# Attention and two dense layers on one core: score tiles of two banks, the last 128 keys of two heads in a common bank, values per query tile in three pieces

## The chip, the core and the metric

The kernel runs on one core of a Trainium2 chip. The metric is the device time of one execution in microseconds (us); the kernel before takes 677.83 us, the median of three executions (676.55 to 678.01). Of the core's engines, PE is TensorE (PEld its weight loads), DVE is VectorE, ACT is ScalarE, POOL is GpSimd and SP is SyncE, which issues most DMAs. Each engine works through its own instructions strictly in the order in which the program issues them; semaphores hold one that needs another engine's result. PSUM has eight banks, each of 512 fp32 values per partition.

## The reference

Pooled attention for 2 x 8 heads of 1152 keys and 576 pooled queries of 64 values, and then two dense layers:

```python
q_pool = q.reshape(B, H, S // 2, 2, D).mean(axis=3)
scores = scale * np.matmul(q_pool, k.transpose(0, 1, 3, 2))
scores = scores - np.max(scores, axis=-1, keepdims=True)
attn = np.exp(scores)
attn = attn / (np.sum(attn, axis=-1, keepdims=True) + 1e-09)
x = np.matmul(attn, v)            # to (1152, 512)
h = x @ w_in                      # 512 -> 2048
g = np.maximum(h, 0.0) + np.log1p(np.exp(-np.abs(h)))
x = g @ w_out                     # 2048 -> 512
h = np.maximum(np.maximum(x @ w1, x @ w2), x @ w3)    # 512 -> 768
out = h @ w_out2                  # 768 -> 512
```

## The kernel before

Heads go in eight pairs. A pair has nine score tiles of 128 rows: four query tiles of 128 for each of its two heads (t = 0 to 3, head i = 0 and 1), and one tail tile that holds the last 64 queries of both. Tile m runs from 0 to 71, nine to a pair.

For each tile, `scores` (L437) makes three PSUM banks of 384 keys each with two matmuls a bank (three in the tail tile); the high and low halves of the operands are kept apart for accuracy. Two such score tiles fit at once (`NS` = 2), six banks. `key_max` (L453) takes the negated maximum over the 1152 keys on DVE, `exps` (L459) makes e = exp(s + nm) on ACT together with the row sum. `turn_e` (L472) transposes e in three groups of three 128 x 128 blocks (`te`), each into one of the two common banks (`NTB` = 2), and `keep_e` (L478) copies each group to `p` in SBUF, on DVE or ACT by the table `ENGINE`.

After four tiles (t = 0 and 1) and after the other five, `finish` (L614) closes a half pair w: `inverse` (L496) makes the reciprocals of the sums, `spread` (L505) spreads them over partitions with matmuls into a common bank (`tr`), `keep_spread` (L530) copies that to `rr`, `values` (L518) multiplies p with v in one run of matmuls into the other common bank (`x`), 256 columns wide for the first half pair and 320 for the second, and `divide` (L541) writes x times rr to `xy`. In `values` and `spread` each head writes one half of the partitions, so their matmuls load 64 columns of weights and two run at once; all other attention matmuls load 128.

While a pair runs, the next one is prepared (`prepare`, L555): q and k are loaded, q is pooled on POOL, both are transposed (`tq`, `tk`) through common banks and split into halves.

The order of all this is not written by hand. Each step is given to `Order.add` (L61) with an engine, a cost and a place (a number of tiles), and `Order.ordered` (L76) plays the steps through: an engine that is free takes the ready step of the lowest place. A step with `take` needs a free common bank, one with `free` gives it back. The instructions are issued in that order.

The conversion of the first ten weight tiles of the dense layers into high and low halves, and the first steps for three more, have places far behind everything else (L635 to L646), so they fill gaps. For each tile n there is a load `raw`, an absolute value on ACT (`size`), a bound on POOL, three integer steps on DVE (L237, L246, L250, into `t`), the high half on ACT (`wh`, L265) and the low half on DVE (`wl`, L270). The first three loads wait for the last keys and queries of the seventh pair, so the conversions begin late in the attention. The dense layers are ordered by a second `Order`, behind all of the above. Their first matmuls are five steps `up` (`bank_h`), and then `down` (`bank_y`), which needs the low half `gl` of the first hidden block from DVE (`low_g`, L755).

Of the kernel before, what the change touches and what calls it, by code (L numbers as in the profile page):

```python
# [8 lines left out]
F32 = mybir.dt.float32  # L9
# [3 lines left out]
ALU = mybir.AluOpType  # L13
# [3 lines left out]
P = 128  # L17
# [7 lines left out]
NBANKS = 7  # L25
NG = 8
NS = 2
NTB = 2
NE = 3

AT = {"max": -1.78, "exp": -0.31, "turn": 0.93, "keep": 0.1, "spread": 4.0, "values": 5.26}
ENGINE = ["DAA", "DDD", "DAA", "DDA", "ADD"]
PREP = {1: -5.28, 2: -7.74, 3: -4.5, 4: -3.31, 5: -1.64}
PREP_AFTER = {0: (0,), 1: (1, 2), 2: (3,), 3: (4,), 4: (5,)}


# [91 lines left out]
def kernel(  # L130
# [153 lines left out]
    def slot(name, n, count):  # L284
        return f"{name}{n % count}"
# [151 lines left out]
    def scores(m, pr, i, t, b):  # L437
        if b == 0:
            tiles["s", m] = ps.tile([P, NB, 512], F32, tag=slot("s", m, NS), name=f"s_{m}")
        sp = tiles["s", m]  # L440
        q1, q2, k1, kl = q1s[pr % 2], q2s[pr % 2], tiles["k1", pr], tiles["kl", pr]
        cols = slice(b * BK, (b + 1) * BK)
        to = sp[:, b, :BK]
# [9 lines left out]
    def key_max(m):  # L453
        tiles["nm", m] = sm.tile([P, 1], F32, tag=slot("nm", m, 3), name=f"nm_{m}")
# [4 lines left out]
    def exps(m, w, x, first):  # L459
        e = pp.tile([P, S], F32, tag=slot("e", m, NE), name=f"e_{m}")  # L460
        if first:
            tiles["sum", w] = sm.tile([P, 5], F32, tag=slot("sum", w, 2), name=f"sum_{w}")
        nc.scalar.activation(  # L463
            out=e.rearrange("p (b s) -> p b s", b=NB),
            in_=tiles["s", m][:, :, :BK],
            func=AF.Exp,
            bias=tiles["nm", m],
            accum_out=tiles["sum", w][:, x : x + 1],
        )
        tiles["e", m] = e  # L470
# [7 lines left out]
    def keep_e(w, i, t, b, n, first, engine):  # L478
        if first:
            tiles["p", w, b] = pp.tile([P, 2, KT, 2 * QB + TAILQ], F32, tag=f"p{b}", name=f"p_{w}_{b}")  # L480
        tp = tiles["t", n]
        if t < NT:
            c0 = (t % 2) * QB
            to = tiles["p", w, b][:, i, :, c0 : c0 + QB]
        else:
            to = tiles["p", w, b][:, :, :, 2 * QB :]
# [6 lines left out]
    def width(w):  # L493
        return 2 * QB if w % 2 == 0 else 2 * QB + TAILQ

    def inverse(w):  # L496
        nx = 4 if w % 2 == 0 else 5
        r = sm.tile([P, 5], F32, tag=slot("r", w, 2), name=f"r_{w}")
        tiles["r", w] = r
        nc.vector.tensor_scalar(  # L500
            out=r[:, :nx], in0=tiles["sum", w][:, :nx], scalar1=1e-9, scalar2=None, op0=ALU.add
        )
        nc.vector.reciprocal(r[:, :nx], r[:, :nx])

    def spread(w, n):  # L505

        r = tiles["r", w]
        tp = bank(n, [P, width(w)], f"tr_{w}")
        for t in range(2):
            for i in range(2):  # L510
                one = r[:, 2 * t + i : 2 * t + i + 1].to_broadcast([P, D])
                nc.tensor.matmul(tp[halves(i), t * QB : (t + 1) * QB], one, ident, start=True, stop=True)
        if w % 2:
            for i in range(2):
                one = r[:, 4:5].to_broadcast([P, D])
                nc.tensor.matmul(tp[halves(i), 2 * QB :], one, ident[:, halves(i)], start=True, stop=True)

    def values(w, n):  # L518
        x = bank(n, [P, width(w)], f"x_{w}")
        for j in range(NJ):  # L520
            for i in range(2):
                nc.tensor.matmul(  # L522
                    x[halves(i)],
                    tiles["v", w // 2][:, i, j],
                    tiles["p", w, j // KT][:, i, j % KT, : width(w)],
                    start=(j == 0),
                    stop=(j == NJ - 1),
                )
# [26 lines left out]
    def prepare(pr, step):  # L555
# [19 lines left out]
        else:  # L575
# [8 lines left out]
            elif g == NB - 1:  # L584
                order.add("SP", 5.6, p, both_k, pr, reads=[f"kh_{b}" for b in range(NB)],
                          writes=[f"k1{y}_{to}{b}" for to in range(2) for b in range(NB)])

    def one_tile(pr, x):
        i, t = (x % 2, x // 2) if x < 2 * NT else (0, NT)
        m = TILES * pr + x  # L590
        w = 2 * pr + (t >= 2)
        y = pr % 2
        sx = 2 * (t % 2) + i if t < NT else 4
        s, e = slot("s", m, NS), slot("e", m, NE)
        banks = [f"{s}_{b}" for b in range(NB)]
        for b in range(NB):
            order.add("PE", 0.35 if t < NT else 0.52, m + b / NB, scores, m, pr, i, t, b,
                      reads=[f"q{z}{y}_{g}" for z in (1, 2) for g in range(2)]
                      + [f"q1{y}_d0", f"q1{y}_d1", f"k1{y}_0{b}", f"k1{y}_1{b}", f"kl{y}_{b}"],
                      writes=(banks[b],) + ((s,) if b == 0 else ()))  # L600
        order.add("DVE", 1.28, m + AT["max"], key_max, m, reads=banks + [s], writes=(slot("nm", m, 3),))
        order.add("ACT", 1.21, m + AT["exp"], exps, m, w, sx, sx == 0,
                  reads=[slot("nm", m, 3), s] + banks, writes=(e, f"sum{w % 2}"))
# [7 lines left out]
        if sx == 3 and t == 1 or t == NT:
            finish(m, w)

    def finish(m, w):  # L614
        nx = 4 if w % 2 == 0 else 5
        y = (w // 2) % 2
        at = m + AT["values"]
        n1, n2 = next_bank(), next_bank()
        order.add("DVE", 0.3, m + 0.3, inverse, w, reads=(f"sum{w % 2}",), writes=(f"r{w % 2}",))
        order.add("PE", 0.6, m + AT["spread"], spread, w, n1, reads=(f"r{w % 2}",), writes=(f"b{n1}",), take=("t", n1))  # L620
        order.add("ACT", 0.36, m + AT["spread"], keep_spread, w, n1, reads=(f"b{n1}",), writes=("rr",), free=("t", n1))
        order.add("PE", 4.0 if w % 2 == 0 else 4.9, at, values, w, n2,
                  reads=[f"p_{x}_{b}" for x in range(nx) for b in range(NB)] + [f"v{y}"],
                  writes=(f"b{n2}", "pw"), take=("t", n2))
        order.add("DVE", 0.4, at - 3, divide, w, n2, reads=(f"b{n2}", "rr"), free=("t", n2))
# [372 lines left out]
```

## Time and profile before

| | |
|---|---|
| median of three executions | 677.83 us (676.55 to 678.01) |
| profiled execution, first to last instruction | 675.7 us |
| attention, to the last `divide` | 309.4 us of it |
| PE busy | 637.5 us, 94% |
| DVE busy | 446.9 us, 66% |
| ACT busy | 351.5 us, 52% |
| POOL busy | 219.6 us, 32% |

The profile gives no other time for the profiled execution than its span. What lies around a span is 2.1 us against the median. In the trace a matmul's row lasts from its start to the modelled end of its pipeline, so rows overlap; what a matmul costs in a run of them is the step from its start to the start of the next. DVE and ACT rows overlap a little in the same way.

### The profile page before, as it was taken

To read this page: it belongs to the slowest core of one execution; us is meant where nothing else is said; L and a number is where in the kernel's file an instruction comes from. 1 tells how busy PE (TensorE), PEld (TensorE's weight loads), DVE (VectorE), ACT (ScalarE), POOL (GpSimd) and SP (SyncE) were. 2 spreads that over 40 slices of the span, in tenths; PEclk is the share of its full clock that TensorE was granted. 3 is DMA by queue.
4 is the path that set the end of the run, shared out by engine and by line. 5 is a ranking of instruction groups with operands and counts; after the bars stand their busy time and mean duration, and the time that the engine had idled before them with its cause. 6 is when DMAs were issued, how large, how long until landed. Compare 5 with 4: busy or idle time off the path is not lost.

```text
span 675.7 us, 10352 instructions
## 1 busy us (share of the span) xinstructions
PE 637.5 (94%) x3914; PEld 556.3 (82%) x3914; DVE 446.9 (66%) x747; ACT 351.5 (52%) x697; POOL 219.6 (32%) x204
## 2 busy tenths in 40 slices
PE   2899999999999998999899999999999999999997
PEld 1676677676767766667799999999999999999996
DVE  3866667667777799985867979797688871111111
ACT  4655555556565666656767676767574431211211
POOL 1100000000000112216987877779695510000000
PEclk9999999999999999999799999999999999999999
DMA  7443433324241735212223333232022310100101
GB/s 191 107 105 89 96 98 73 100 69 98 68 99 43 198 116 164 94 64 81 76 63 97 122 98 122 94 126 93 32 94 95 124 32 1 47 1 1 47 1 48
DMA packets 56546, 56.87 MB, mean 84 GB/s; under 512 B 21168, under 2 KB 47792, under 8 KB 56496
## 3 DMA queue, kind: packets, MB, share of 16 engines
q1 hardware_dynamic: 55280, 55.62, 28.8%
q10 hardware_dynamic: 1216, 0.59, 0.3%
q8 instruction: 31, 0.51, 0.3%
q14 instruction: 19, 0.16, 0.1%
HBM read 43.52 MB, written 2.36 MB: 68 GB/s over the span
## 4 chain that ended last, share of the span: by engine, by line
PE 78%; DVE 10%; ACT 6%; issue 2%; DMA 2%; POOL 2%; SPq 0%; ACTq 0%; DVEq 0%; POOLq 0%
PE bank_h_m L675 17%; PE bank_h L675 15%; PE bank_y L675 14%; PE x L522 9%; PE te L476 7%; PE bank_o L675 6%; DVE nm L455 4%; PE s L446 4%; ACT e L463 4%; DVE p L491 3%; PE s L447 3%; DMA k<-in_k_dram 2%; ACT p L489 1%; PE tk L348 1%; PE s L449 1%
## 5 line engine op out<-in xcount | busy, mean ns | idle before, releaser
L226 POOL TENSOR_SCALAR size<-size 128x512 f32<-128x512 f32 x56 | 84.3, 1507 | 98.9 <-ACT size L221 98.7
L675 PE MATMUL bank_h_m<-x,wh 128*128 128x384 f32 x432 | 114.6, 339 | 0.0
L476 PE MATMUL te<-ident,e 128*128 128x128 f32 x648 | 101.8, 282 | 11.2 <-DVE p L491 7.8
L455 DVE TENSOR_REDUCE nm<-s 128x1 f32<-128x1152 f32 x72 | 97.4, 1352 | 14.7 <-PE s L447 12.5
L675 PE MATMUL bank_h<-x,wh 128*128 128x384 f32 x384 | 106.3, 339 | 0.2 <-DVE gl L757 0.2
L476 PEld LDWEIGHTS te<-ident,e 128*128 128x128 f32 x648 | 73.1, 140 | 38.8 <-DVE p L491 20.1
L463 ACT ACTIVATE e<-s,nm 128x1152 f32<-128x1152 f32 x72 | 88.3, 1226 | 22.0 <-DVE nm L455 17.0
L675 PEld LDWEIGHTS bank_h_m<-x,wh 128*128 128x128 f32 x432 | 78.9, 188 | 0.8
L446 PE MATMUL s<-k,q 128*128 128x384 f32 x192 | 76.1, 396 | 3.1 <-ACT e L463 3.1
L489 ACT COPY p<-te 128x384 f32<-128x384 f32 x88 | 39.7, 482 | 72.0 <-PE te L476 71.8
L491 DVE COPY p<-te 128x384 f32<-128x384 f32 x128 | 66.5, 552 | 11.7 <-PE te L476 9.9
L522 PE MATMUL x<-p,v 128*64 128x320 f32 (+1 forms) x576 | 73.3, 408 | 0.0
L675 PE MATMUL bank_h_m<-x,wl 128*128 128x384 f32 x216 | 73.1, 338 | 0.0
L675 PEld LDWEIGHTS bank_h<-x,wh 128*128 128x128 f32 x384 | 70.3, 188 | 1.1 <-DVE gl L757 0.6
L675 PE MATMUL bank_y<-gh,wh 128*128 128x384 f32 x192 | 66.1, 344 | 3.7 <-ACT gh L752 3.7
L333 POOL TENSOR_TENSOR qs<-q 128x512 f32<-128x512 f32 x7 | 8.9, 1273 | 185.7 <-PE tq L401 166.5
L675 PE MATMUL bank_y<-gl,wh 128*128 128x384 f32 x192 | 65.9, 343 | 0.1
L675 PE MATMUL bank_y<-gh,wl 128*128 128x384 f32 x192 | 65.8, 343 | 0.0
L447 PE MATMUL s<-kl,q 128*128 128x384 f32 x192 | 65.4, 341 | 0.0
L675 PE MATMUL bank_h<-x,wl 128*128 128x384 f32 x192 | 65.0, 339 | 0.0
L522 PEld LDWEIGHTS x<-p,v 128*64 128x64 f32 x576 | 39.9, 137 | 28.2 <-issue 2.3
L733 POOL TENSOR_TENSOR d<-e,d 128x384 f32<-128x384 f32 x48 | 49.0, 1022 | 29.1 <-DVE d L726 26.5
(216 smaller groups left out, 1096.9 us busy)
## 6 DMA issues: line engine op xcount, KB each, us to landing
raw<-in_moe_w_out_dram SPq DMA_DIRECT2D x22, 512.0 KB, 3.3
raw<-in_moe_w_dram SPq DMA_DIRECT2D x18, 512.0 KB, 3.5
raw<-in_moe_w_in_dram SPq DMA_DIRECT2D x16, 512.0 KB, 3.8
k<-kh SPq DMA_DIRECT2D x28, 288.0 KB, 5.8
k<-in_k_dram SPq DMA_DIRECT2D x16, 288.0 KB, 4.5
v<-in_v_dram SPq DMA_DIRECT2D x16, 288.0 KB, 3.2
q<-in_q_dram SPq DMA_DIRECT2D x14, 256.0 KB, 3.2
out_dram<-ob SPq DMA_DIRECT2D x9, 256.0 KB, 2.0
```

The lines of the kernel that those rows point to most:

```text
L226: nc.gpsimd.tensor_scalar(out=size, in0=size, scalar1=SMALLEST, scalar2=None, op0=ALU.max)
L333: engine.tensor_tensor(out=qs.rearrange("p t i d -> p i t d"), in0=q1[:, :, :, 0], in1=q1[:, :, :, 1], op=ALU.add)
L446: nc.tensor.matmul(to, q1[:, i, at1 : at1 + QB], k1[:, i, cols], start=True, stop=False)
L447: nc.tensor.matmul(to, q2[:, at2 : at2 + QB], kl[:, cols], start=False, stop=True)
L455: nc.vector.tensor_reduce(out=tiles["nm", m], in_=tiles["s", m][:, :, :BK], axis=AX.XY, op=ALU.max, negate=True)
L463: nc.scalar.activation(out=e.rearrange("p (b s) -> p b s", b=NB), in_=tiles["s", m][:, :, :BK], func=AF.Exp, bias=tiles["nm", m], accum_ou ...
L476: nc.tensor.transpose(tp[:, t], tiles["e", m][:, j * P : (j + 1) * P], ident)
L489: nc.scalar.copy(to, tp)
L491: nc.vector.tensor_copy(to, tp)
L522: nc.tensor.matmul(x[halves(i)], tiles["v", w // 2][:, i, j], tiles["p", w, j // KT][:, i, j % KT, : width(w)], start=(j == 0), stop=(j == ...
L675: nc.tensor.matmul(ps, lhs(a, kk), rhs(bb, kk), start=start and n == 0, stop=stop and n == last)
L733: nc.gpsimd.tensor_tensor(out=d, in0=gs["e", i], in1=d, op=ALU.subtract)
```

## The change

A score tile has two banks of 512 keys, for the first 1024 keys (`NM` = 2, `SB` = 512). The scores of the last 128 keys (`NR`) of both heads of a query tile go together into one common bank (`rest_scores`, tile `sr`); there are four common banks (`NTB` = 4). `rest_max` takes the maxima of the rest of both heads, `key_max` that of the 1024 keys, and a second instruction of it joins the two. `exps` makes the first 1024 columns of e, and `rest_exps` the last 128, with a sum of its own. A half pair is gone: each query tile t of a pair of heads is one w (40 instead of 16), `p` is kept twice (`NP` = 2), and `values` runs in three pieces of 384 keys, whose x is 128 columns wide (64 in the tail). `spread` writes beside x into the same bank. The planner's places and some costs are other numbers. The dense layers are as before.

```diff
-NTB = 2
+NTB = 4
+NP = 2
+SB = 512
...
+    def rest_scores(w, pr, t, n):
+        tp = bank(n, [P, heads(t), NR], f"sr_{w}")
+        for i in range(heads(t)):
+            score(tp[:, i], pr, i, t, slice(NM * SB, S))
+
+    def rest_max(w, t, n):
+        tiles["nr", w] = sm.tile([P, 2], F32, tag=slot("nr", w, 2), name=f"nr_{w}")
         nc.vector.tensor_reduce(
-            out=tiles["nm", m], in_=tiles["s", m][:, :, :BK], axis=AX.XY, op=ALU.max, negate=True
+            out=tiles["nr", w][:, : heads(t)], in_=tiles["t", n], axis=AX.X, op=ALU.max, negate=True
+        )
+
+    def key_max(m, w, i):
+        nm = sm.tile([P, 2], F32, tag=slot("nm", m, 3), name=f"nm_{m}")
+        nc.vector.tensor_reduce(out=nm[:, 1:], in_=tiles["s", m], axis=AX.XY, op=ALU.max, negate=True)
+        nc.vector.tensor_tensor(out=nm[:, :1], in0=nm[:, 1:], in1=tiles["nr", w][:, i : i + 1], op=ALU.min)
...
+    def rest_exps(m, w, i, n):
+        nc.scalar.activation(
+            out=tiles["e", m][:, NM * SB :],
+            in_=tiles["t", n][:, i],
+            func=AF.Exp,
+            bias=tiles["nm", m],
+            accum_out=tiles["sum", w][:, 1, i : i + 1],
+        )
...
-            tiles["p", w, b] = pp.tile([P, 2, KT, 2 * QB + TAILQ], F32, tag=f"p{b}", name=f"p_{w}_{b}")
+            tiles["p", w, b] = pp.tile([P, 2, KT, QB], F32, tag=f"p{b}{w % NP}", name=f"p_{w}_{b}")
...
-    def values(w, n):
-        x = bank(n, [P, width(w)], f"x_{w}")
-        for j in range(NJ):
+    def values(w, t, b, n):
+        if b == 0:
+            bank(n, [P, 2, QB], f"x_{w}")
+        x = tiles["t", n][:, 0, : width(t)]
+        for j in range(b * KT, (b + 1) * KT):
...
+    def spread(w, t, n):
+        r, tp = tiles["r", w], tiles["t", n][:, 1, : width(t)]
+        for i in range(2):
+            one = r[:, i : i + 1] if t < NT else r[:, :1]
+            unit = ident if t < NT else ident[:, halves(i)]
+            nc.tensor.matmul(tp[halves(i)], one.to_broadcast([P, D]), unit, start=True, stop=True)
...
+        for b in range(NB):
+            at = m + AT["values"] + b * AT["step"]
+            order.add("PE", 0.67 if t < NT else 0.4, at, values, w, t, b, n,
+                      reads=[f"p{y2}_{i}_{b}" for i in range(heads(t))] + [f"v{y}"],
+                      writes=(f"b{n}", f"pw{y2}{b}"), take=("t", n) if b == 0 else None)
+        order.add("PE", 0.3, at + 0.01, spread, w, t, n, reads=(f"r{w % 2}",), writes=(f"b{n}",))
```

How the order moves is seen at three places. The first is PE around a run of values in the third pair. In the names, the number behind te, s or e is the tile m, that behind x, p, tr or r is w, and the last one only counts buffers. Before:

```order
L451 MATMUL s_26_1126<-kl_2_735,q2_0_98 128x384
L348 MATMUL tk_3_2_1136<-ident_91,k_3_795 128x128 x3
L522 MATMUL x_4_1140<-p_4_0_994,v_2_662 64x256 x6
L522 MATMUL x_4_1140<-p_4_1_1004,v_2_662 64x256 x6
L522 MATMUL x_4_1140<-p_4_2_1011,v_2_662 64x256 x6
L476 MATMUL te_22_0_1169<-ident_91,e_22_1052 128x128 x3
L449 MATMUL s_26_1126<-k1_2_799,q1_0_97 128x384
L476 MATMUL te_22_1_1179<-ident_91,e_22_1052 128x128 x3
L476 MATMUL te_22_2_1185<-ident_91,e_22_1052 128x128 x3
L476 MATMUL te_23_0_1193<-ident_91,e_23_1080 128x128 x3
```

And with the change:

```order
L501 MATMUL te_21_0_1312<-ident_91,e_21_1278 128x128 x3
L540 MATMUL x_10_1316<-p_10_0_1174,v_2_779 64x128 x6
L540 MATMUL x_10_1316<-p_10_1_1181,v_2_779 64x128 x6
L501 MATMUL te_21_1_1340<-ident_91,e_21_1278 128x128 x3
L447 MATMUL s_23_1303<-k1_2_980,q1_0_97 128x512
L448 MATMUL s_23_1303<-kl_2_889,q2_0_98 128x512
L540 MATMUL x_10_1316<-p_10_2_1202,v_2_779 64x128 x6
L351 MATMUL tk_3_0_1354<-ident_91,k_3_954 128x128 x3
L501 MATMUL te_21_2_1361<-ident_91,e_21_1278 128x128 x3
L553 MATMUL x_10_1316<-ident_91,r_10_1222 64x128 x2
```

Where one run of 18 rows' worth of values stood, and nine groups of transposes in a row behind it, pieces of values now stand singly between transposes and scores.

The second place is DVE at a query tile of the fourth pair, with the change (before, each of the two maxima was one row):

```order
L466 TENSOR_REDUCE nr_15_1591<-sr_15_1584 128x2
L472 TENSOR_REDUCE nm_27_1599<-s_27_1577 128x1
L473 TENSOR_TENSOR nm_27_1599<-nm_27_1599,nr_15_1591 128x1
L521 COPY p_14_2_1613<-te_26_2_1595 128x6x64
L472 TENSOR_REDUCE nm_28_1618<-s_28_1604 128x1
```

Three instructions stand where one stood, and the copies of p wait behind all of them.

The third place is DVE around the last division of the attention. Before, with the low half of the tenth weight tile (`wl_9`) far ahead of it:

```order
L543 TENSOR_TENSOR xy_96<-x_14_3008,rr_14_2999 128x256
L270 TENSOR_TENSOR wl_9_3057<-t_9_3039,wh_9_3056 128x512
L455 TENSOR_REDUCE nm_71_3079<-s_71_3047 128x1
...
L543 TENSOR_TENSOR xy_96<-x_15_3157,rr_15_3176 128x320
L237 TENSOR_SCALAR t_10_3212<-size_10_3035 128x512
```

And with the change:

```order
L273 TENSOR_TENSOR wl_6_4056<-t_6_4005,wh_6_4055 128x512
L564 TENSOR_TENSOR xy_96<-x_38_3997,rr_38_4079 128x128
L564 TENSOR_TENSOR xy_96<-x_39_4044,rr_39_4083 128x64
L253 SCALAR_TENSOR_TENSOR t_7_4066<-raw_7_3844,t_7_4066 128x512
L240 TENSOR_SCALAR t_8_4088<-size_8_4068 128x512
...
L273 TENSOR_TENSOR wl_9_4115<-t_9_4101,wh_9_4114 128x512
L240 TENSOR_SCALAR t_10_4156<-size_10_4109 128x512
```

The conversions of three weight tiles, 7 to 9, have moved from ahead of the last division to behind it.

## Rows read from the trace of the kernel before

**Rows 1.** The page: the span.

```profile
span 675.7 us, 10352 instructions
```

**Rows 2.** Busy time by stretch: PE, PEld, DVE, ACT, POOL, clock, DMA share, GB/s.

```profile
100.00:140.00 40.00, 38.41 (x271) 28.60 (x269) 29.13 (x45) 21.90 (x42) 1.68 (x2) 1.00 0.35 88
260.00:300.00 40.00, 36.59 (x262) 27.19 (x260) 38.41 (x63) 28.53 (x53) 10.98 (x7) 1.00 0.34 108
```

**Rows 3.** Chain that ended last: start, length, what. Second value runs of pairs two, five.

```profile
92.70 4.99 PE x L522 x36
...
199.70 5.00 PE x L522 x36
```

**Rows 4.** PE in order of time, 90 to 99 us: start, us, line, tiles.

```profile
90.25 0.66 PE L512 MATMUL tr<-ident,r 128*64 128x128 f32 x8
90.73 0.28 PE L516 MATMUL tr<-ident,r 128*64 128x64 f32 x4
90.95 0.44 PE L446 MATMUL s<-k,q 128*128 128x384 f32 x1
...
92.63 5.07 PE L522 MATMUL x<-p,v 128*64 128x320 f32 x36
97.62 0.55 PE L476 MATMUL te<-ident,e 128*128 128x128 f32 x3
...
98.36 0.33 PE L446 MATMUL s<-k,q 128*128 128x384 f32 x1
...
98.71 0.82 PE L476 MATMUL te<-ident,e 128*128 128x128 f32 x6
```

**Rows 5.** PE in order of time, 111 to 123 us.

```profile
111.60 4.11 PE L522 MATMUL x<-p,v 128*64 128x256 f32 x36
115.63 0.55 PE L476 MATMUL te<-ident,e 128*128 128x128 f32 x3
...
121.47 0.43 PE L446 MATMUL s<-k,q 128*128 128x384 f32 x1
...
121.92 0.49 PE L476 MATMUL te<-ident,e 128*128 128x128 f32 x3
...
122.60 0.49 PE L476 MATMUL te<-ident,e 128*128 128x128 f32 x3
```

**Rows 6.** PE in order of time: the last two matmuls of that run.

```profile
115.32 0.39 PE L522 MATMUL x<-p,v 128*64 128x256 f32 x2
```

**Rows 7.** PE in order of time: scores, then the start of a run of values.

```profile
236.64 0.34 PE L447 MATMUL s<-kl,q 128*128 128x384 f32 x1
236.91 0.49 PE L522 MATMUL x<-p,v 128*64 128x320 f32 x2
```

**Rows 8.** DVE by line, to 330 us: count, busy us, mean ns, idle before.

```profile
L455 DVE TENSOR_REDUCE nm<-s 128x1 f32<-128x1152 f32 x72 | 97.4, 1352 | 14.7 <-PE s L447 12.5 <-PE s L451 2.1
L491 DVE COPY p<-te 128x384 f32<-128x384 f32 x128 | 66.5, 552 | 11.7 <-PE te L476 9.9
L543 DVE TENSOR_TENSOR xy<-x,rr 128x256 f32<-128x256 f32 x8 | 3.4, 422 | 17.4 <-PE x L522 17.4
L503 DVE RECIPROCAL r<-r 128x4 f32<-128x4 f32 x8 | 1.4, 178 | 0.3
```

**Rows 9.** ACT by line, to 330 us.

```profile
L463 ACT ACTIVATE e<-s,nm 128x1152 f32<-128x1152 f32 x72 | 88.3, 1226 | 22.0 <-DVE nm L455 17.0 <-PE te L476 4.2
```

**Rows 10.** PE in order of time: the first score matmuls of the program.

```profile
18.80 0.52 PE L446 MATMUL s<-k,q 128*128 128x384 f32 x1
19.12 0.52 PE L447 MATMUL s<-kl,q 128*128 128x384 f32 x1
```

**Rows 11.** DVE in order of time, end of attention; idle time before and its releaser in brackets.

```profile
302.60 1.02 DVE L491 COPY p<-te 128x384 f32<-128x384 f32 x2 [1.29 <-PE te L476]
308.95 0.49 DVE L543 TENSOR_TENSOR xy<-x,rr 128x320 f32<-128x320 f32 x1 [5.32 <-PE x L522]
```

**Rows 12.** PE in order of time: the first `down` of the dense layers.

```profile
323.29 0.69 PE L675 MATMUL bank_y<-gh,wh 128*128 128x384 f32 x1 [3.67 <-ACT gh L752]
```

More of the change, by code (lines that the diff above doesn't have):

```diff
@@ L27 @@
 NS = 2
-NTB = 2
+NTB = 4
 NE = 3
-AT = {"max": -1.78, "exp": -0.31, "turn": 0.93, "keep": 0.1, "spread": 4.0, "values": 5.26}
+NP = 2
+SB = 512
+AT = {"rest": -0.46, "max": -2.87, "exp": -2.8, "turn": 0.92, "keep": -1.54, "values": 3.16, "step": 0.7,
+      "spread": 3.28}
 ENGINE = ["DAA", "DDD", "DAA", "DDA", "ADD"]
-PREP = {1: -5.28, 2: -7.74, 3: -4.5, 4: -3.31, 5: -1.64}
+PREP = {1: -5.34, 2: -7.91, 3: -4.48, 4: -3.15, 5: -3.77}
 PREP_AFTER = {0: (0,), 1: (1, 2), 2: (3,), 3: (4,), 4: (5,)}
@@ L435, in both_q, with score @@
         nc.sync.dma_start(q1[D:, 1, TAILQ:], q2[D:, NQ:])
[L437 to L440, printed above, removed]
+    NM = S // SB
+    NR = S - NM * SB
+    def score(to, pr, i, t, cols):
         q1, q2, k1, kl = q1s[pr % 2], q2s[pr % 2], tiles["k1", pr], tiles["kl", pr]
-        cols = slice(b * BK, (b + 1) * BK)
-        to = sp[:, b, :BK]
         if t < NT:
@@ L463, in exps @@
+    def exps(m, w, i):
+        tiles["e", m] = pp.tile([P, S], F32, tag=slot("e", m, NE), name=f"e_{m}")
+        if i == 0:
+            tiles["sum", w] = sm.tile([P, 2, 2], F32, tag=slot("sum", w, 2), name=f"sum_{w}")
         nc.scalar.activation(
-            out=e.rearrange("p (b s) -> p b s", b=NB),
-            in_=tiles["s", m][:, :, :BK],
+            out=tiles["e", m][:, : NM * SB].rearrange("p (b s) -> p b s", b=NM),
+            in_=tiles["s", m],
             func=AF.Exp,
             bias=tiles["nm", m],
-            accum_out=tiles["sum", w][:, x : x + 1],
+            accum_out=tiles["sum", w][:, 0, i : i + 1],
@@ L476, in turn_e, with heads, width, keep_e @@
             nc.tensor.transpose(tp[:, t], tiles["e", m][:, j * P : (j + 1) * P], ident)
[L478 to L480 removed]
+    def heads(t):
+        return 2 if t < NT else 1
+    def width(t):
+        return QB if t < NT else TAILQ
+    def keep_e(w, i, t, b, n, engine):
+        if i == 0:
+            tiles["p", w, b] = pp.tile([P, 2, KT, QB], F32, tag=f"p{b}{w % NP}", name=f"p_{w}_{b}")
         tp = tiles["t", n]
         if t < NT:
[L483 to L484 removed]
+            to = tiles["p", w, b][:, i]
         else:
[L486 removed]
+            to = tiles["p", w, b][:, :, :, :TAILQ]
             tp = tp.rearrange("p t (i s) -> p i t s", i=2)
@@ L491, in keep_e, with inverse @@
             nc.vector.tensor_copy(to, tp)
[L493 to L498, printed above, removed]
+    def inverse(w, t):
+        nx = heads(t)
+        r = sm.tile([P, 2], F32, tag=slot("r", w, 2), name=f"r_{w}")
         tiles["r", w] = r
-        nc.vector.tensor_scalar(
-            out=r[:, :nx], in0=tiles["sum", w][:, :nx], scalar1=1e-9, scalar2=None, op0=ALU.add
+        s = tiles["sum", w]
+        nc.vector.scalar_tensor_tensor(
+            out=r[:, :nx], in0=s[:, 0, :nx], scalar=1e-9, in1=s[:, 1, :nx], op0=ALU.add, op1=ALU.add
         )
         nc.vector.reciprocal(r[:, :nx], r[:, :nx])
[L505 to L516, printed above, removed]
-    def values(w, n):
-        x = bank(n, [P, width(w)], f"x_{w}")
-        for j in range(NJ):
+    def values(w, t, b, n):
+        if b == 0:
+            bank(n, [P, 2, QB], f"x_{w}")
+        x = tiles["t", n][:, 0, : width(t)]
+        for j in range(b * KT, (b + 1) * KT):
             for i in range(2):
@@ L594, in one_tile, with ks @@
         s, e = slot("s", m, NS), slot("e", m, NE)
[L595 to L603, printed above, removed]
+        qs = [f"q{z}{y}_{g}" for z in (1, 2) for g in range(2)] + [f"q1{y}_d0", f"q1{y}_d1"]
+        def ks(a, z):
+            return [f"{k}_{to}{g}" if k[1] == "1" else f"{k}_{g}"
+                    for k, to in ((f"k1{y}", 0), (f"k1{y}", 1), (f"kl{y}", 0))
+                    for g in range(a // BK, (z - 1) // BK + 1)]
+        if i == 0:
+            n = rests[w] = next_bank()
+            p = m + AT["rest"]
+            order.add("PE", 0.44 if t < NT else 0.33, p, rest_scores, w, pr, t, n,
+                      reads=qs + ks(NM * SB, S), writes=(f"b{n}",), take=("t", n))
+            order.add("DVE", 0.3 if t < NT else 0.2, p, rest_max, w, t, n, reads=(f"b{n}",), writes=(f"nr{w % 2}",))
+        n = rests[w]
+        banks = [f"{s}_{b}" for b in range(NM)]
+        for b in range(NM):
+            order.add("PE", 0.475 if t < NT else 0.71, m + b / NM, scores, m, pr, i, t, b,
+                      reads=qs + ks(b * SB, (b + 1) * SB), writes=(banks[b],) + ((s,) if b == 0 else ()))
+        nm = slot("nm", m, 3)
+        order.add("DVE", 1.25, m + AT["max"], key_max, m, w, i, reads=banks + [s, f"nr{w % 2}"], writes=(nm,))
+        order.add("ACT", 1.08, m + AT["exp"], exps, m, w, i, reads=[nm, s] + banks, writes=(e, f"sum{w % 2}"))
+        order.add("ACT", 0.31, m + AT["exp"], rest_exps, m, w, i, n, reads=[nm, f"b{n}"],
+                  writes=(e + "r", f"sum{w % 2}"), free=("t", n) if i == heads(t) - 1 else None)
+        y2 = w % NP
         for b in range(NB):
@@ L611, in one_tile @@
[L611 to L625, printed above, removed]
+                      keep_e, w, i, t, b, n, engine,
@@ new lines, in one_tile, with finish @@
+                      reads=(f"b{n}",), writes=(f"p{y2}_{i}_{b}",), free=("t", n))
+        if i == heads(t) - 1:
+            finish(m, w, t)
+    def finish(m, w, t):
+        y, y2 = (w // (NT + 1)) % 2, w % NP
+        n = next_bank()
+        order.add("DVE", 0.3, m + 0.3, inverse, w, t, reads=(f"sum{w % 2}",), writes=(f"r{w % 2}",))
+        for b in range(NB):
[4 more added lines that the diff above has]
+        order.add("PE", 0.3, at + 0.01, spread, w, t, n, reads=(f"r{w % 2}",), writes=(f"b{n}",))
+        at += AT["spread"]
+        order.add("ACT", 0.3, at, keep_spread, w, t, n, reads=(f"b{n}",), writes=(f"rr{w % 2}", f"b{n}"))
+        order.add("DVE", 0.3, at, divide, w, t, n, reads=(f"b{n}", f"rr{w % 2}"), free=("t", n))
```

43 lines of the change are left out of this document (20 added, 23 removed).

## The prediction

> **What bounds the kernel now.** I read the page first: the span is 675.7 us [rows 1], 2.1 us under the median of 677.83, and I sum against the span and carry the difference to the median. Next the busy time by stretch. In the middle of the attention PE is busy 38.4 of 40 us, DVE 29.1 and ACT 21.9; near its end, where the weight conversions fill gaps, DVE has 38.4 of 40 [rows 2]. So the attention is PE's, with DVE beside it at the end. The dense layers behind it are untouched, and they start to count when their first `down` starts: there PE stood idle for 3.67 us, waiting for ACT and, behind it, DVE [rows 12]. What the change is worth is therefore how much earlier that `down` can start.
>
> A busy PE is not a PE at its peak, so I take steps from start to start. A pair of heads lasts (199.70 - 92.70) / 3 = 35.7 us [rows 3]. Prices: a score matmul of 384 keys (98.71 - 98.36) / 2 = 0.175; three transposes and two score matmuls together 122.60 - 121.92 = 0.68, so a group of three transposes 0.33; a run of values 115.63 - 111.60 = 4.03 and 97.62 - 92.63 = 4.99; the spreading of sums 0.48, with a tail 0.70 [rows 4, 5]. A pair has 57 score matmuls (10.0 us), 27 groups te (8.9), 3 groups tk (1.0), 5 blocks tq (0.55), two runs of values (9.0), two spreads (1.2), and four entries into such runs at 0.1, priced below (0.4). That is 31.1 us of work: 4.6 of the 35.7 are lost. Where, rows 5 show: the scores at 121.47 start 5.84 us after the run of values ended at 115.63, with only 27 transposes (2.97) and three score matmuls (0.53) between. 2.3 us are lost in one place, where nine groups te in a row wait for copies to empty two common banks. The rest is smaller waits of the same kind, and waits of scores for exp.
>
> **The change, part by part.**
>
> *Scores.* 38 matmuls of 512 keys and 19 of 128 replace 57 of 384. At the same price per key the long one costs 0.175 x 512 / 384 = 0.233. No row has a short one. Its columns alone are 0.175 x 128 / 384 = 0.06; at most it costs as much as a long one's 0.175, if loading 128 columns of weights sets it. A te block, also 128 columns under 128 columns of weights, steps by 0.11, and I take that as the nearest [rows 4, 5]. 38 x 0.233 + 19 x 0.11 = 10.9: +1.0 us a pair, between 0.0 and +2.2. The Trainium skill (TensorE: Matmul & The Clock Gate, section Back-to-back issue gap) gives about 81 ns for a sustained load-and-multiply of 128 columns. By that the rest would cost 1.5 instead of 2.1 us a pair, and +0.4 would stand for the +1.0; no row here shows such a step.
>
> *Values and spread in pieces.* The columns stay the same, 576 a pair. A step of two matmuls 256 wide is (115.32 - 111.60) / 17 = 0.219 [rows 5, 6]; by the two runs' difference, 64 columns cost (4.99 - 4.03) / 18 = 0.053, so 0.006 of a step does not depend on width. There are 90 steps instead of 36: +0.3 us. What costs is going in and out of them. From the last step to the next transpose 115.63 - 115.32 = 0.31, which is 0.09 over a step [rows 5, 6]; from a score matmul into a run 236.91 - 236.64 = 0.27, which is 0.10 over its 0.175 [rows 7]. So each separate stretch of 64-column matmuls costs 0.19. The order has 31 such stretches before and 112 now, 14 a pair instead of 3.9: 81 x 0.19 = 15 us in all, +1.9 a pair.
>
> *So PE's work* goes from 31.1 to 34.3 us a pair, and the change pays only if most of the 4.6 lost go.
>
> *The lost time.* The batch of nine groups behind a run of values is gone from the order: te, scores and pieces of values alternate, so copies have work of PE's beside them. I laid PE's, DVE's and ACT's instructions of the fourth pair side by side with these prices. sr and x hold a bank each for about two tiles and te has the other two, but its copies return them in time; PE waited only for a bank in front of x_13 and sr_16 and for exp in front of te_35, together 0.4 us. So 34.7 us a pair, 1.0 less than now. Between lie nothing lost (34.3) and all lost time kept (38.9). Five pairs run in this state (the second to the sixth): -5.0 us.
>
> *DVE.* A maximum over 128 keys fewer: per column (1352 - 422) / (1152 - 256) = 1.04 ns, so 1.22 us for 1.35, -1.2 a pair. Added: 9 joins like the reciprocal's 0.18 (1.6), rest maxima of 256 columns as the division's 0.42 and one of 0.28 (2.0), three more inverses of two instructions (1.1), three more divisions at their fixed part of 0.16 (0.5) [rows 8]. +4.0, of which 0.8 overlaps, as two copies of 0.55 fit in 1.02 [rows 8, 11]: +3.2 a pair. Through the middle this is hidden: 29.1 of 40 us become about 33. What is queued behind the join is the copies of p; they come 0.1 later, te waits for them, and that is in the 0.4.
>
> *ACT.* A second exp with its own sum per tile: nearest row 1.23 for 1152 keys [rows 9]; some 0.3 net a tile, 3 us a pair, hidden by 18 idle us of 40 [rows 2]. It delays only the third te group of a tile. Uncovered, it would add its 3 us.
>
> *Start.* The first maximum now waits for eight short and four long score matmuls instead of six of 384. Here these step by 19.12 - 18.80 = 0.32, 1.8 times the later price [rows 10]: 8 x 0.2 + 4 x 0.43 = 3.3 against 1.9, +1.4 us.
>
> *End.* The conversions start with the last key and query copies of the seventh pair, so they move with the pairs. From the first of them to the first `gl`, DVE now has 16 tiles of +3.2 / 9 each: +5.7 us. Conversions 7 to 9 stand behind the last division instead of ahead of it; this is no work more, only a place. Against it, DVE idled 1.29 and 5.32 us there while PE ran te and the last values [rows 11]; now it has some 7 us of copies and conversions under the last exp, te, values and division, which follow in less, so I take 5 back. +0.7 us. SP's queue has the same 132 rows in nearly the same order, so DMAs cost nothing.
>
> **Sum.** -5.0 + 1.4 + 0.7 = -2.9 us: a span of 672.8 and a time of **675.0 us**.
>
> **The rivals.**
>
> *PE is full* (slower). Most of the wait stays and the 112 switches are paid: the place is te behind its copies, with DVE's joined maximum ahead of them. If only the 2.3 us of rows 5 go, a pair takes 34.3 + 2.3 = 36.6: +0.9, five pairs +4.5, with start and end +6.6: 684.4. It decides from 3.2 us recovered downwards. For it: PE's added work is read from rows, the recovery is argued. Against it: the order has no batch left. The Trainium skill (TensorEngine Tiling (Array Packing), section Key Properties) says that a change of tiling mode drains TensorE. If a drain were a te row's whole tail, 0.27 less 0.11 each way, 81 stretches would cost 11 us more than I count; rows 6 and 7 show less than that.
>
> *Cheap rests and a full end* (much faster). The short matmuls cost their columns, 0.06: 0.9 a pair, over eight pairs -7, and 668 us. For it: weights load beside the matmul ahead. Against it: te's 0.11.
>
> *Nothing gained.* sr and x hold two of the four banks, so te has two, as before, and the loss shrinks just by what PE's work grows: +1.4 + 0.7 and some 0.5 a pair, about 677.5.
>
> **How the numbers follow.** The forecast has 0.40, its own range 670 to 679; PE is full 0.27; cheap rests 0.18; nothing gained 0.15. Within 0.2%, 1.4 us, nothing can be told from no change. Faster: 0.33 of the forecast, 0.17 of cheap rests, 0.02 of nothing gained, 0.52. Same: 0.06, 0.10 of nothing gained, 0.16. Slower: 0.32. The range reaches past cheap rests on one side and to a price of 0.175 for them or a full PE on the other: 664 to 687.
>
> **What would show it.** Right: 14 stretches of values a pair with 0.1 before and behind each; a pair of 34 to 35 us from x to x; steps of 0.11 between sr matmuls and 0.23 between the long ones; nm at 1.22; the first `down` some 3 us earlier, with a longer idle time of PE ahead of it; te waits for p nearly gone from PE. Wrong: te still waiting for p more than 1.5 us a pair, sr steps away from 0.11, or DVE idle before the last division.

## The result: slower, 685.93 us

The changed kernel takes 685.93 us (median of 4 runs, 685.03 to 686.9), the kernel before 677.5 beside it: ratio 1.0125, 95% interval 1.0108 to 1.0143. I forecast 675.0 and faster. The time lies inside the range, beside the 684.4 of the rival "PE is full".

The page after, first the span [rows 1], then busy time by engine:

```profile
span 683.1 us, 12417 instructions
...
PE 653.4 (96%) x4778; PEld 583.1 (85%) x4778; DVE 472.9 (69%) x931; ACT 374.4 (55%) x865; POOL 219.7 (32%) x204
```

Busy time by stretch, the changed kernel (columns as in [rows 2]; the first two stretches are those of [rows 2], the others the end of the attention):

```profile
100.00:140.00 40.00, 40.00 (x382) 31.77 (x382) 30.60 (x68) 25.88 (x68) 2.44 (x3) 1.00 0.40 98
260.00:300.00 40.00, 39.99 (x384) 31.51 (x383) 37.09 (x84) 27.97 (x71) 6.06 (x5) 1.00 0.28 77
...
307.00:316.00 9.00, 0.26 (x10) 0.12 (x5) 7.88 (x14) 4.18 (x8) 4.55 (x4) 0.66 0.52 164
316.00:320.00 4.00, 2.72 (x7) 2.06 (x8) 2.82 (x5) 3.80 (x10) 4.00 (x4) 0.50 0.54 181
```

The lost time is gone, as forecast: PE is busy 40.00 of 40 us, where it had 38.41. But the pair did not become shorter. VectorE in order of time, the changed kernel: the maxima that open pairs 2, 5 and 6 (counted from 0), and the last two divisions:

```profile
87.86 1.23 DVE L472 TENSOR_REDUCE nm<-s 128x1 f32<-128x1024 f32 x1
...
196.90 1.22 DVE L472 TENSOR_REDUCE nm<-s 128x1 f32<-128x1024 f32 x1
...
233.25 1.22 DVE L472 TENSOR_REDUCE nm<-s 128x1 f32<-128x1024 f32 x1
...
307.67 0.41 DVE L564 TENSOR_TENSOR xy<-x,rr 128x128 f32<-128x128 f32 x2
```

A pair lasts (196.90 - 87.86) / 3 = 36.35 us, against 35.7 [rows 3]: +0.65, where I had -1.0. Still the last division ends at 308.08, 1.4 us earlier than before's 308.95 + 0.49 [rows 11]. The time is lost behind it. TensorE in order of time, the changed kernel, first a piece of the middle, then the seam to the dense layers:

```profile
162.30 0.40 PE L448 MATMUL s<-kl,q 128*128 128x512 f32 x1
162.63 1.53 PE L540 MATMUL x<-p,v 128*64 128x128 f32 x24
164.09 0.50 PE L447 MATMUL s<-k,q 128*128 128x512 f32 x1
164.43 0.40 PE L448 MATMUL s<-kl,q 128*128 128x512 f32 x1
164.66 0.39 PE L447 MATMUL s<-k,q 128*128 128x512 f32 x1
164.89 0.40 PE L448 MATMUL s<-kl,q 128*128 128x512 f32 x1
...
166.02 0.28 PE L448 MATMUL sr<-kl,q 128*128 128x128 f32 x1
166.13 0.28 PE L447 MATMUL sr<-k,q 128*128 128x128 f32 x1
166.25 0.27 PE L448 MATMUL sr<-kl,q 128*128 128x128 f32 x1
...
306.97 0.29 PE L553 MATMUL x<-ident,r 128*64 128x64 f32 x4
316.16 0.69 PE L718 MATMUL bank_h<-x,wh 128*128 128x384 f32 x1 [8.90 <-ACT x L827]
...
330.99 0.34 PE L718 MATMUL bank_y<-gh,wh 128*128 128x384 f32 x1
```

The first `down` comes at 330.99 instead of 323.29 [rows 12], and from there to the end of the span nothing changed (352.1 us, before 352.4). So the whole loss of the span is in front of it, and TensorE stands idle for 8.90 us there, waiting for ScalarE's casts of x. What stands ahead of those casts, ScalarE in order of time:

```profile
308.71 0.62 ACT L268 CAST wh<-t 128x512 fp32r<-128x512 f32 x1 [1.14 <-DVE t L253]
...
311.39 0.62 ACT L268 CAST wh<-t 128x512 fp32r<-128x512 f32 x1 [1.49 <-DVE t L253]
...
314.52 0.62 ACT L268 CAST wh<-t 128x512 fp32r<-128x512 f32 x1 [1.34 <-DVE t L253]
...
315.61 2.15 ACT L827 CAST x<-xy 128x384 fp32r<-128x384 f32 x5
```

Three weight conversions, each waiting for VectorE's words `t`, stand in ScalarE's queue ahead of the casts.

Two theories follow. **A, the tail**: the loss is these conversions behind the last division. **B, the switches**: entering and leaving 64-column matmuls costs more than I counted, the pair is long for that, and the tail only follows.

### The profile page after: what moved, and what is told of

Read it like the earlier page. It is cut to its first block, busy times and chain, and to the rows that moved or that the text cites. A ratio compares the mean times of both kernels' runs of the same rounds, so it can differ in the third digit from the quotient of the medians.

```text
span 683.1 us, 12417 instructions
## 1 busy us (share of the span) xinstructions
PE 653.4 (96%) x4778; PEld 583.1 (85%) x4778; DVE 472.9 (69%) x931; ACT 374.4 (55%) x865; POOL 219.7 (32%) x204
## 3 DMA queue, kind: packets, MB, share of 16 engines
q1 hardware_dynamic: 55280, 55.62, 29.3%
## 4 chain that ended last, share of the span: by engine, by line
PE 90%; DVE 3%; POOL 2%; DMA 2%; issue 1%; ACT 1%; SPq 0%; POOLq 0%; DVEq 0%; ACTq 0%
PE bank_h_m L718 17%; PE bank_y L718 14%; PE bank_h L718 13%; PE x L540 11%; PE te L501 11%; PE bank_o L718 6%; PE s L447 6%; PE s L448 4%; PE x L553 2%; DMA k<-in_k_dram 2%; PE tk L351 2%; PE sr L448 1%; PE sr L447 1%; POOL size L229 1%; PE s L450 1%
## 5 line engine op out<-in xcount | busy, mean ns | idle before, releaser
L718 PE MATMUL bank_h<-x,wh 128*128 128x384 f32 x384 | 108.5, 345 | 11.1 <-ACT x L827 8.9
L480 ACT ACTIVATE e<-s,nm 128x1024 f32<-128x1024 f32 x72 | 80.5, 1118 | 21.0 <-DVE nm L473 17.6
L472 DVE TENSOR_REDUCE nm<-s 128x1 f32<-128x1024 f32 x72 | 87.6, 1217 | 4.3 <-PE s L448 3.1
L540 PE MATMUL x<-p,v 128*64 128x128 f32 (+1 forms) x1440 | 89.7, 268 | 0.0
L521 DVE COPY p<-te 128x384 f32<-128x384 f32 x128 | 68.8, 552 | 27.7 <-PE te L501 27.2
L540 PEld LDWEIGHTS x<-p,v 128*64 128x64 f32 x1440 | 71.7, 137 | 18.7 <-issue 8.7
L501 PEld LDWEIGHTS te<-ident,e 128*128 128x128 f32 x648 | 72.5, 141 | 17.2 <-issue 7.7
L519 ACT COPY p<-te 128x384 f32<-128x384 f32 x88 | 41.4, 481 | 51.6 <-PE te L501 51.0
L447 PE MATMUL s<-k,q 128*128 128x512 f32 x128 | 60.1, 469 | 1.7 <-ACT e L480 1.7
L849 DVE TENSOR_TENSOR mg<-bank_h_m,mg 128x384 f32<-128x384 f32 x18 | 10.0, 556 | 61.7 <-PE bank_h_m L718 61.7
```

Of the source, the lines that this page charges most:

```text
L472: nc.vector.tensor_reduce(out=nm[:, 1:], in_=tiles["s", m], axis=AX.XY, op=ALU.max, negate=True)
L480: nc.scalar.activation(out=tiles["e", m][:, : NM * SB].rearrange("p (b s) -> p b s", b=NM), in_=tiles["s", m], func=AF.Exp, bias=tiles["nm ...
L540: nc.tensor.matmul(x[halves(i)], tiles["v", w // (NT + 1)][:, i, j], tiles["p", w, b][:, i, j % KT, : width(t)], start=(j == 0), stop=(j = ...
L718: nc.tensor.matmul(ps, lhs(a, kk), rhs(bb, kk), start=start and n == 0, stop=stop and n == last)
```

## The experiments

Pairs are counted from opening maximum to opening maximum, "tail" is from the end of the last division to the first `down`. All ratios are against the kernel before, with 95% intervals.

### One: seven conversions in the attention

```diff
-NPRE = 10
+NPRE = 7
```

> Seven weight conversions instead of ten are planned into the attention; numbers 7 to 9 go to the dense layers' own order. Theory A (the loss is in the tail: in the changed kernel ScalarE's first casts of x stand at 315.61 us behind conversions 7 to 9 that wait for VectorE, while the attention itself ends at 308.08, 1.4 us earlier than before): the first up-projection starts within 2 us of the last value matmul, at 307 to 309.5 us instead of 316.16, the first down-projection at 321 to 324 instead of 330.99, time 676 to 679 us. Theory B (the loss is TensorE's switching in the pair, 36.35 us instead of 35.6, and the tail only follows from it): VectorE's work is only moved a few us on, the dense layers wait for it there instead, time 684 to 687 us. Under both the pair stays at 36.3 to 36.4 us.

Measured: 678.71 us, ratio 1.0022 (1.0011 to 1.0033), 7.2 us under the change. TensorE in order of time:

```profile
307.86 0.29 PE L553 MATMUL x<-ident,r 128*64 128x64 f32 x4
308.92 0.44 PE L718 MATMUL bank_h<-x,wh 128*128 128x384 f32 x1 [0.78 <-ACT x L827]
...
323.02 0.44 PE L718 MATMUL bank_y<-gh,wh 128*128 128x384 f32 x1 [1.17 <-ACT gh L795]
```

The idle time before the first up-projection falls from 8.90 to 0.78 us. A holds for the tail; the pair stays at 36.35, so the kernel is still not faster than before.

### Two: the ten conversions entered early

```diff
     for step in range(6):
         prepare(0, step)
+    for n in range(NPRE + 3):
+        ...
     for pr in range(NPAIR):
...
-    for n in range(NPRE + 3):
-        ...
```

> The ten conversions are entered into the plan right behind the first pair's preparation, so that their loads wait for pair 0's copies and not for pair 6's, and VectorE and ScalarE can do them anywhere in the attention. Theory A: none of them stands behind the last division, the first down-projection comes 13 to 15 us after the last division instead of 22.9, time 675 to 679 us. Theory B: the same work in the pairs delays the copies of the turned exponentials there, and what the tail gains the pairs lose: pairs of 36.8 us and more where conversions lie, time 682 to 687 us.

Measured: 677.32 us, 1.0006 (0.9992 to 1.0021). TensorE by stretch:

```profile
100.00:172.00 72.00, 72.00 (x707) 57.12 (x706) 62.37 (x136) 49.25 (x126) 9.32 (x8) 1.00 0.48 121
172.00:245.00 73.00, 73.00 (x708) 57.80 (x707) 56.13 (x123) 45.12 (x118) 3.37 (x4) 1.00 0.35 83
```

The tail is 14.4 us instead of 22.9. TensorE now has no gap between pair 2 and the dense layers, and the kernel only equals the one before. What keeps it there is TensorE's own work, so B has to be tried.

### Three and four: the value pieces and the spread in one step

```diff
-        for b in range(NB):
-            ...
-            order.add("PE", 0.67 if t < NT else 0.4, at, values, w, t, b, n, ...)
-        order.add("PE", 0.3, at + 0.01, spread, w, t, n, ...)
+        at = m + AT["values"] + (NB - 1) * AT["step"]
+        order.add("PE", 2.3 if t < NT else 1.5, at, all_values, w, t, n, ...)
```

> The three value pieces of a query tile and its spread are one step of TensorE: 39 stretches of 64-column matmuls instead of 112, the same matmuls. Theory B (each stretch costs 0.25 to 0.30 us of TensorE, of which the second long step behind its end is a part): 73 stretches fewer, 9 a pair, take 2.3 to 2.7 us off a pair, 36.35 to 33.7 to 34.1 us, attention 18 to 22 us shorter, time 664 to 670 us. Rival (the waits for copies that the pieces filled come back, as in the kernel before, since up to six turns now follow each other): lost time rises from under 1 to 2.5 us a pair and more, pair 35.5 to 36.5 us, time 677 to 686 us. Theory A alone: the attention gets shorter, but the conversions behind it keep the distance from the last division to the first down-projection at 23 us or more.

> The two edits together: value pieces and spread in one step, conversions entered behind pair 0's preparation. If A and B both hold, the two gains add: the pair of the joined kernel (33.7 to 34.1 us by B, 35.5 to 36.5 by the rival of returning waits) and the first down-projection 13 to 15 us behind the last division: 655 to 662 us, or 668 to 677 us by the rival. If conversions in the pairs bring the copies late, it is no faster than the joined kernel alone.

Measured: 680.64 us, 1.0052 (1.0033 to 1.0072), and with early conversions 680.8, 1.0052 (1.0036 to 1.0067). TensorE by stretch, without the early conversions:

```profile
100.00:172.00 72.00, 69.31 (x709) 58.06 (x705) 55.95 (x123) 44.48 (x118) 3.38 (x4) 1.00 0.37 92
172.00:245.00 73.00, 68.24 (x672) 56.79 (x672) 56.45 (x125) 46.39 (x121) 7.69 (x7) 1.00 0.43 109
```

TensorE does have less to do, but it idles 2.7 and 4.8 us, and the pair is about 36.1. The rival of returning waits won. Up to eighteen transposes stand between two value steps now, but it is not shown that their copies alone set the pace: of the 7.5 us the trace puts 1.7 down to copies of p and 1.9 to `exp`, and 3.3 lie ahead of rest scores without a releaser that can be trusted. The tail is 16.1 us, where A alone had 23 or more: nine of the ten conversions are done before the last division here, seven in the change. The early conversions add nothing here; pairs 0 to 2 lasted 38.1, 37.4 and 37.0 us with them.

### Five and six: two steps, cut in two places

```diff
-        for b in range(NB):
-            ...
-        order.add("PE", 0.3, at + 0.01, spread, ...)
+        for bs in PIECES:
+            at = m + AT["values"] + bs[-1] * AT["step"]
+            last = bs[-1] == NB - 1
+            order.add("PE", (0.67 if t < NT else 0.4) * len(bs) + 0.3 * last, at, some_values, w, t, bs, n, ...)
```

`PIECES` is [[0, 1], [2]] in five and [[0], [1, 2]] in six; the spread goes with the last; conversions early in both.

> As the run with the conversions entered early (677.32 us, pairs 35.7 to 36.35), but the values of a query tile in two steps instead of three: the first two blocks of 384 keys together, the last block with the spread: 76 stretches of 64-column matmuls instead of 112. Theory B (between the changed kernel and the joined one the value, spread and neighbouring steps of two pairs sum to 29.3 us in 30 stretches and 22.8 in 10, 0.33 us a stretch): 4.5 stretches fewer a pair, 1.5 us less work, pair 34.6 to 35.3 us, time 665 to 671 us. Rival (waits for the copies come back as fast as switches go, as in the joined kernel, where TensorE was idle 2.7 of 72 us): pair 35.8 to 36.4, time 676 to 679 us.

> The same with the cut elsewhere: the first block alone, the last two with the spread; the plan puts 61 stretches. Theory B: 6.4 stretches fewer a pair than with three steps, 2.1 us less work, pair 34.1 to 35.0, time 661 to 669 us. Rival: longer steps leave less to fill a wait with, lost time of 1.5 us and more a pair, time 672 to 679 us.

Measured: five 700.4 us, 1.0338 (1.0322 to 1.0353); six **666.68 us, 0.9843** (0.9826 to 0.9859). VectorE in order of time, six:

```profile
159.19 1.23 DVE L473 TENSOR_REDUCE nm<-s 128x1 f32<-128x1024 f32 x1
...
262.27 1.22 DVE L473 TENSOR_REDUCE nm<-s 128x1 f32<-128x1024 f32 x1
```

That is (262.27 - 159.19) / 3 = 34.36 us a pair; pairs 1 and 2, with conversions in them, took 36.2 and 35.8. TensorE by stretch, six and then five:

```profile
172.00:245.00 73.00, 72.52 (x752) 60.53 (x752) 59.54 (x129) 48.00 (x125) 3.38 (x4) 1.00 0.37 86
```

```profile
172.00:245.00 73.00, 65.92 (x642) 52.34 (x641) 54.91 (x114) 43.27 (x112) 3.37 (x4) 1.00 0.28 64
```

Six has fewer switches with TensorE still full; B holds there. Five missed both expectations: its order makes TensorE wait 7.1 of 73 us, most of all scores for `exp` and values for VectorE, and the pair grows to 39.3 us. Which step of that order is to blame I did not pursue. It warns that the number of switches alone decides nothing: the order they come in must keep TensorE fed.

### Seven: the score part alone

Values, spread and division as in the kernel before, per half pair, on top of the changed scores; the edit is that code of before put back, with the sums still inverted per query tile.

> The score part of the change alone: two score banks, the last 128 keys of two heads in a common bank, four common banks; values, spread and division per half pair as in the kernel before (16 stretches). My price for the score part was 1.0 us of TensorE a pair and nothing else. Theory B (the dear part is the switching of the value pieces): work 32 to 32.5 us a pair, lost time at most the 4.6 of before, less where two more banks shorten the nine turns behind the small value run: pair 34.0 to 36.5 us, time 664 to 682 us. Rival (the score part is the dear one, by its short matmuls and the second exponential of each head): pair over 36.5 us and time over 684 us.

Measured: 678.13 us, 1.001 (1.0001 to 1.002). VectorE in order of time, the maxima opening pairs 1 and 7:

```profile
51.48 1.22 DVE L472 TENSOR_REDUCE nm<-s 128x1 f32<-128x1024 f32 x1
...
269.58 1.22 DVE L472 TENSOR_REDUCE nm<-s 128x1 f32<-128x1024 f32 x1
```

Over these six pairs that is 36.35 us a pair: four took 35.1 to 35.5, near before's 35.6, and two over 38, in which TensorE waited. The stretches are 31, as before (the 16 in the expectation are half pairs). The rival of dear scores falls, since it wanted over 684 us: the score part neither costs nor brings much. The other 7.8 us of the change came with the values in pieces, the tail included (here it is 13.6).

### Eight to ten: where the conversions lie

Eight is six with the conversions where the change has them. Nine lets them in two or three at a time, after each second pair. Ten is the kernel before with the block of conversions moved as in two.

> The kernel of 666.68 us (values of a query tile in two steps, the first block alone, the last two with the spread) but with the conversions where the change has them, entered last and loaded from pair 6 on. Theory A (what does not fit into the last two pairs stands between the last division and the first down-projection): the attention ends no later than there, at 296 to 298.5 us, the first down-projection 21 to 26 us behind it instead of 14.4: time 673 to 678 us. If the conversions fit into two pairs after all, or the tail follows from the longer pair alone (theory B for the tail), 666 to 669 us.

> The same two steps with the conversions let in two or three at a time, after each second pair, instead of all ten in pairs 0 to 2. In the kernel of 666.68 us the pairs with conversions took 36.19 and 35.84 us, those without 34.03 to 34.53. If the crowding costs that (copies of turned exponentials late behind four conversions a pair), pairs of 34.3 to 35 us throughout and 663 to 666 us; if each conversion costs its share wherever it lies, 666 to 668 us.

> The kernel before with its conversions entered behind pair 0's preparation, nothing else. There the first up-projection already follows the last value matmul within 0.4 us, so theory A gives it nothing: 675 to 680 us. If the conversions in its last two pairs delay copies there (its lost time is 4.6 us a pair with and without them), no gain either; a gain of over 3 us would say that the early conversions by themselves, and not the tail of the changed kernel, are what the faster kernels live on.

Measured: eight 674.34 us, 0.9955 (0.994 to 0.9969); nine 668.63, 0.9861 (0.9826 to 0.9896); ten 687.24, 1.0138 (1.0116 to 1.0159). Eight, TensorE in order of time:

```profile
305.85 0.69 PE L725 MATMUL bank_h<-x,wh 128*128 128x384 f32 x1 [9.41 <-ACT x L834]
...
320.64 0.34 PE L725 MATMUL bank_y<-gh,wh 128*128 128x384 f32 x1
```

The tail is back in eight (22.3 us) although its pairs last 34.6: A does not need the long pair. Nine missed its hope: its two worst pairs took 36.9 and 37.1 us. Ten missed its 675 to 680, and shows that early conversions are no gift of their own. VectorE in order of time, ten, pairs 1 and 2:

```profile
55.10 1.35 DVE L455 TENSOR_REDUCE nm<-s 128x1 f32<-128x1152 f32 x1
...
97.70 1.35 DVE L455 TENSOR_REDUCE nm<-s 128x1 f32<-128x1152 f32 x1
```

One pair with conversions took 42.6 us there. The kernel before bears them worse than six does; why is not shown.

### Eleven and twelve: two steps and seven conversions

Six's two steps with `NPRE = 7`, the conversions late (eleven) and early (twelve).

> The two-step values with seven conversions in the attention instead of ten, entered last as in the change. It puts the two causes together without crowding pairs 0 to 2. With pairs of 34.0 to 35.0 us (as without early conversions) the attention ends at 297 to 299.5 us; theory A: the first down-projection 14 to 15 us behind, dense layers 1.3 us longer (350.6 instead of 349.3 us, as with seven conversions before): 663 to 668 us. If three conversions fewer leave a tail of over 18 us, A is wrong about which work it is: 670 us and more.

> The same with the seven conversions entered early, in pairs 0 and 1. Against the 666.68 us of ten early ones: three conversions fewer to crowd pair 2, about 1.3 us back for 1.3 us more in the dense layers: 664 to 668 us, not told apart from it if the two terms are as said.

Measured: **666.61 us, 0.984** (0.9823 to 0.9858), and 666.86, 0.9846 (0.9825 to 0.9868). TensorE in order of time, eleven:

```profile
297.27 0.44 PE L725 MATMUL bank_h<-x,wh 128*128 128x384 f32 x1 [0.78 <-ACT x L834]
...
311.69 0.44 PE L725 MATMUL bank_y<-gh,wh 128*128 128x384 f32 x1 [1.15 <-ACT gh L802]
```

The dense layers did not grow by the 1.3 us I expected: from the first `down` to the last instruction they take 352.4 us, against 352.1 in eight. Six, eleven and twelve can't be told apart; all beat both kernels by about 1.6 and 2.8%. With the change, one and eight, eleven closes a square:

| | ten conversions, late | seven |
|---|---|---|
| three steps and spread (112 stretches) | 685.93 | 678.71 |
| two steps (63 stretches) | 674.34 | 666.61 |

The tail is worth 7.2 and 7.7 us, the switches 11.6 and 12.1: each is worth the same whatever the other is. Both theories name something that costs time, side by side. The 49 stretches fewer would give 16.2 us at the 0.33 derived below; part of that goes in waits, as TensorE idles 1.8 of the 145 us from 100 to 245 in eight and not at all in the change.

## Why the prediction was wrong

**The step that failed is the price of a stretch**, in "Values and spread in pieces": "So each separate stretch of 64-column matmuls costs 0.19." It measured 0.33. The rows at 162 to 165 us above price it. Into values: 162.63 - 162.30 = 0.33, 0.10 over a long step's 0.23; that I had. Twelve steps of two matmuls and out: 164.09 - 162.63 = 1.46, where twelve steps at 0.11 are 1.31: 0.15. And the *second* score matmul comes after 164.43 - 164.09 = 0.34 instead of 0.23, 0.11 more; that I had not looked for. Together 0.36 us with scores behind. With transposes behind, the same second-step excess is 0.055 (0.164 instead of 0.109) and the stretch costs about 0.30. Over two pairs, all start-to-start steps of values and spread, with what the step into a stretch and the second one behind it take beyond their usual price, give 29.3 us in the change's 30 stretches and 22.8 in the joined kernel's 10: 0.33 a stretch. My exit had been read from a 256-column run, and only to the first transpose behind it. The Trainium skill (TensorEngine Tiling (Array Packing), Key Properties) says that a change of tiling mode drains TensorE; the trace agrees that both ends of a stretch cost, 0.30 to 0.36 us in all, though no row shows the drain itself. The rival that I built on it, 0.16 each way, had the right size, and I dismissed it by rows that stop one step too early.

My 34.3 us of work hold the fourteen stretches of a pair at about 0.19. At 0.33 they are 2.0 us more: 36.3, and 36.35 was measured. The 0.4 us of waits in my 34.7 did not come: from 100 to 240 us the trace lists no wait of TensorE's. Eight is a check by itself: 63 stretches at 0.33 are 20.8 us, as 112 at 0.19 are 21.3. It is nearly the kernel that I had priced, and it runs pairs of 34.6 us (forecast 34.7) and 674.34 us (forecast 675.0).

Where the span went, by the maxima that open pairs 1 and 6, VectorE in order of time, before and then the changed kernel (its pair 6 stands above):

```profile
49.88 1.36 DVE L455 TENSOR_REDUCE nm<-s 128x1 f32<-128x1152 f32 x1 [0.62 <-PE s L447]
...
230.46 1.36 DVE L455 TENSOR_REDUCE nm<-s 128x1 f32<-128x1152 f32 x1 [0.47 <-PE s L447]
```

```profile
51.52 1.22 DVE L472 TENSOR_REDUCE nm<-s 128x1 f32<-128x1024 f32 x1
```

The five pairs between take 181.7 us, before 180.6: +1.2 where I had -5.0. The start is +1.6 for +1.4, the end, from pair 6's opening to the first `down`, +4.9 for +0.7. In eight the end is only +1.3, so 3.6 of the 4.9 follow from the change's longer last two pairs. The span was missed by 10.3 us. The price of a stretch made the five pairs 8.2 us longer than I had them (36.35 for 34.7) and the end 3.6; against that, before's second pair took 38.0 us and not my 35.7, which hides some 2 us of it.

Point by point:

- *Lost time*: right. PE's idle time in the middle of the attention went from 1.6 of 40 us to none, with no wait for p left.
- *Scores*: right. Long steps 0.23 (164.66 to 164.89), short ones 0.11 to 0.12 (166.02 to 166.25); the "cheap rests" rival, at 0.06, falls with them. The Trainium skill (TensorE: Matmul & The Clock Gate, Back-to-back issue gap) has about 81 ns for sustained matmuls of 128 columns, which is not reached here.
- *VectorE and ACT*, by line, the changed kernel to 330 us:

```profile
L472 DVE TENSOR_REDUCE nm<-s 128x1 f32<-128x1024 f32 x72 | 87.6, 1217 | 4.3 <-PE s L448 3.1 <-ACT p L519 0.3 <-PE s L452 0.2
...
L473 DVE TENSOR_TENSOR nm<-nm,nr 128x1 f32<-128x1 f32 x72 | 14.5, 202 | 2.5
L466 DVE TENSOR_REDUCE nr<-sr 128x2 f32<-128x256 f32 x32 | 13.5, 422 | 10.7 <-PE sr L448 10.1
...
L480 ACT ACTIVATE e<-s,nm 128x1024 f32<-128x1024 f32 x72 | 80.5, 1118 | 21.0 <-DVE nm L473 17.6 <-DVE r L528 2.5 <-PE te L501 0.2
...
L489 ACT ACTIVATE e<-sr,nm 128x128 f32<-128x128 f32 x72 | 26.1, 363 | 0.0
```

  nm 1.22 as forecast, the join 0.20 for 0.18, the rest maximum 0.42, all hidden. The second exp is 0.36 and stayed hidden.
- *Start*: the first maximum came no later (20.26, before 20.32), but the first pair took 31.3 us for 29.6. The size was nearly right, +1.7 for +1.4, the reason given was not.
- *End*: two large terms. From pair 6's opening to the last division the change takes 74.8 us, before 79.0, and most of that difference stays where no conversion lies in the stretch (74.2 in experiment two, 77.6 in ten); the tail is 22.9 us, before 13.9. My "this is no work more, only a place" hid what the place is: behind the last division nothing of TensorE's covers a conversion, and the casts of x stand behind it in ScalarE's queue. Moving three of them away brings 7.2 and 7.7 us. So theory A names a place to gain time, but only a small part of what the forecast missed.
- *Rivals*: "PE is full" gave the sign and, within 1.5 us, the time, but by luck: it kept 2.3 us of waiting a pair, and no such wait is in the trace. TensorE was full of switches.

## What to carry to other kernels

Read the price of a switch of matmul shape over the whole detour, from the last step of the old kind to the second step after the return, and not from its two edges. Cutting a long step so that it fills gaps pays only while the gaps are dearer than the cuts: here two steps of a query tile, cut behind the first block, beat both three and one, and the same two cut behind the second lost to both. Where filler work is laid beside a busy engine, look whether anything still covers what is left over at the end, and what is queued behind it.

## What I had not expected of the hardware

- The second matmul after a run of 64-column ones is late too: 0.34 us instead of 0.23 for 512 keys, 0.164 instead of 0.109 for a transpose. (A second long score also starts late, by 0.32, where transposes end without a switch; but there the first one starts 0.03 after the last transpose, and the two steps sum to the usual 0.11 + 0.23.)
- After TensorE's 8.9 us of idle time its granted clock was 0.50 from 316 to 320 us (the lower of its two levels, 1.2 GHz); it was 1.00 up to 307. It cost little: first up-projection to first `down` took 14.83 us, and 14.10 in experiment one, whose clock was 1.00 there, but whose up-projections waited four times for POOL's part of x, 1.0 us in all.
- TensorE at 40.00 of 40 us busy was the slower kernel, and the one at 72.5 of 73 was 2.8% faster: the page counts a switch as busy time.
